# Attention in units of two pairs of heads, with the score matmuls of a pair issued in turn, and the third block's combinations held behind the first expert unit

## The chip, the core and the metric

The kernel runs on one NeuronCore of a Trainium2 chip. Its engines work from queues of their own and wait for one another by semaphores: TensorE (PE, with its weight loads shown as PEld), VectorE (DVE), ScalarE (ACT), GpSimd (POOL), and SyncE (SP), which issues most transfers. The metric is the device time of one execution in microseconds (us).

## What is computed

Three layers follow one another, all in fp32: attention over a band, a gated feed-forward layer, and eight experts of which every token takes a weighted sum.

```python
scores = q @ k.T / sqrt(64) - slope[head] * dist        # 2 batches, 8 heads, 768 tokens
scores = where(is_global | is_local, scores, -1e9)      # the first 8 keys, and the 96 up to the token
a = exp(scores - scores.max(-1)); a = a / (a.sum(-1) + 1e-9)
x = (a @ v)                                             # to 1536 tokens x 512
h = x @ w_in; x = (h * sigmoid(h)) @ w_out              # 512 -> 2048 -> 512
P = exp(x @ w_gate - max); 8 rounds of P /= rows, P /= columns, P *= N / E
for e in range(8): out += P[:, e:e+1] * (maximum(x @ w1[e], 0) @ w2[e])   # 512 -> 1024 -> 512
```

## The kernel before

**Precision.** A product of two fp32 matrices is made of three matmuls of a one-pass format (fp32r): each operand is split into a high part and the rest, and high x high, high x low and low x high are added (`three`, L241 to L243; L280; L407; L442). The high part is made by ScalarE, the rest by VectorE or GpSimd.

**Stages.** The 1536 tokens are three blocks of 512 for the second and third layers, and twelve blocks of 128 queries (k = 0 to 11) for attention. `banded` runs attention for k = 0 and 1 alone, then weaves the rest into the feed-forward layer: k = 2, 3 and then 4 to 7 while the first 512 tokens go through w_in (h, L241) and w_out (y, L280), and k = 8 to 11 while the second 512 do. In the first block VectorE also turns the two weight matrices from 64-bit numbers to fp32 (`narrow`, L203 to L209: 16 pieces of eight operations). `finish` runs the third 512 tokens, and then `layer2` runs the experts.

**An attention unit.** `attention` runs through units; unit (k, j) has the heads 2c + j of all four pairs c, that is one half of every pair. Of a pair the first head's 64 features lie on partitions 0 to 63, the second's on 64 to 127, so all of a unit's score matmuls (`att_scores`, L747) read the same 64 partitions. Two pairs share one PSUM bank of tag "a", of which there are three while attention is woven in; scores, transposes of q and k (L715), of the probabilities (`att_flip`, L785) and the product with v (`att_out`, L804) take turns in them. For blocks 8 to 11 the scores are three fp32r matmuls (kT qT, kTl qT, kT qTl), for the others one fp32 matmul, which the profile shows as two instructions. Then, for each head, VectorE adds the bias and takes the extreme (L756), ScalarE takes the exponential (L760), VectorE makes the reciprocal of the sum (L765, L766), GpSimd multiplies (L768). The flips of a unit come two units later, `att_out` when both units of its block are flipped.

**The experts.** A unit u of `layer2` is one half of an expert's hidden features for one of the three blocks of tokens. Its first matrix is applied by seven products of halves instead of eight (`h_product`, L407), for which the tokens' features are combined beforehand: `x_combine` subtracts quarter tiles (L336) and splits seven of them (L340 on ScalarE, L341 on VectorE), for the first two blocks during the feed-forward layer, and for the third from `rest`, a generator that `window` draws on from unit 1 on. The third block's combinations are needed by unit 2. Within a unit VectorE adds the products' banks (L489, L493, L429) and makes the low parts of what is split (`h_split`, L422); the banks are free for later products when it has read them.

**Order.** The kernel's text gives each instruction a place; a scheduler then sets each engine's order from it by its own estimates, and an instruction that it thinks ready early may stand ahead of its place in the text. Each engine runs its list strictly in order. `tc.issue_after(ins)` holds what is issued in its block behind `ins` on the engine of `ins`, and adds no semaphore.

Of the kernel before, what the change touches and what calls it, by code (L numbers as in the profile page):

```python
# [8 lines left out]
F32 = mybir.dt.float32  # L9
# [11 lines left out]
P = 128  # L21
# [23 lines left out]
def f32(ap):  # L45
    return ap.bitcast(F32)


class Kernel:
# [368 lines left out]
    def h_split(self, src):  # L418

        hi, lo = self.h_room()  # L420
        self.nc.scalar.activation(hi, src, AF.Relu)  # L421
        self.nc.vector.scalar_tensor_tensor(lo, src, 0.0, f32(hi), op0=ALU.max, op1=ALU.subtract)  # L422
        return tuple(x.rearrange("p (f t) -> p f t", f=2) for x in (hi, lo))
# [305 lines left out]
    def att_scores(self, k, j):  # L729
# [5 lines left out]
        jj = slice(j * self.D, (j + 1) * self.D)  # L735
        a["s", j] = s = pool.tile([P, 4, W], F32, tag="s", name=f"s_{k}_{j}", bufs=LAG + 1)
        st = pool.tile([P, 3, 4], F32, tag="st", name=f"st_{k}_{j}", bufs=LAG + 2)
        cols = []
        for c in range(self.NPAIR):
            th = self.tab[2 * c + j]  # L740
            if c % 2 == 0:
                bank = self.aps(f"s_{k}_{j}_{c}")
                for x in (c, c + 1):
                    dst = bank[:, x % 2 * W:x % 2 * W + n]
                    ops = ((0, 0), (0, 1), (1, 0))[:3 if len(qT) > 1 else 1]
                    for i, (y, z) in enumerate(ops):
                        nc.tensor.matmul(  # L747
                            dst, qT[y][jj, x * P:(x + 1) * P], kT[z][jj, x, W - n:],
                            start=i == 0, stop=i == len(ops) - 1,
                        )  # L750
            ps = bank[:, c % 2 * W:c % 2 * W + n]
            tt = th[:, :W] if n == W else th[:, W:]
            sx = s[:, c, W - n:]
            cols.append(sx)

            nc.vector.tensor_tensor_reduce(  # L756
                out=sx, in0=ps, in1=tt, scale=1.0, scalar=BIGMIN, op0=ALU.add, op1=ALU.min,
                accum_out=st[:, 0, c:c + 1],
            )
            nc.scalar.activation(  # L760
                sx, sx, AF.Exp, bias=st[:, 0, c:c + 1], scale=-1.0, accum_out=st[:, 1, c:c + 1]
            )
            if c % 2 == 1:
                two = slice(c - 1, c + 1)
# [423 lines left out]
```

## Time and profile before

| | us |
|---|---|
| median of 3 runs (lowest, highest) | 1426.16 (1425.91, 1428.12) |
| the profiled execution, its own time | 1426.18 |
| its span, first to last instruction | 1424.4 |
| PE busy in the span | 1395.1 (98%) |
| VectorE, ScalarE, GpSimd busy | 731.1, 489.9, 550.9 |

PE is the busiest engine in the mean, but the stages differ: the first 160 us hold attention, the narrowing of the weights and the first block's feed-forward layer, and there VectorE is busy nearly throughout; from then on PE is. The chain that ended last is PE work for 89% of the span. An idle stretch of PE, or work taken from it, is read from the stage in which it lies. The granted clock of PE has two levels here, 2.4 GHz (PEclk 1.0) and 1.2 GHz (0.5).

### The profile page before, as it was taken

How to read it: one execution, taken by the hardware profiler on the slowest of the kernel's cores; microseconds unless marked ns; L12 is line 12 of the kernel's file. 1: busy time of each engine (PE TensorE's matmuls, PEld its weight loads, DVE VectorE, ACT ScalarE, POOL GpSimd, SP SyncE). 2: the span in 40 equal slices, each digit the busy share in tenths (PEclk: the TensorE clock that was granted, in tenths of full speed). 3: DMA queues.
4: the chain of work that ended last, by engine and by line, in shares of the span. 5: the costliest groups of instructions: out<-in, count | busy, mean ns of one | idle time of the engine just before them, and what ended most of it. 6: DMA issues, size and time to landing. Idle time of an engine off the chain costs nothing.

```text
span 1424.4 us, 21277 instructions
## 1 busy us (share of the span) xinstructions
PE 1395.1 (98%) x8552; PEld 1218.0 (86%) x8552; DVE 731.1 (51%) x1298; ACT 489.9 (34%) x949; POOL 550.9 (39%) x489
## 2 busy tenths in 40 slices
PE   8998999999998999999999999999999999999998
PEld 6776677778888998999899989998998899899987
DVE  7899545456235457444444444444444444444443
ACT  6665545555453332222232222222222222222220
POOL 5677756444472424324143331424324142432210
PEclk8999999999999999999999999999999999999999
DMA  9686442212230001010111201011010101101001
GB/s 261 178 249 185 148 119 88 75 61 89 89 110 10 31 30 45 30 45 30 30 30 30 60 16 45 30 30 45 21 55 16 45 31 31 46 30 30 1 31 62
DMA packets 75293, 92.19 MB, mean 65 GB/s; under 512 B 30640, under 2 KB 49072, under 8 KB 75184
## 3 DMA queue, kind: packets, MB, share of 16 engines
q1 hardware_dynamic: 72880, 82.34, 19.3%
q10 hardware_dynamic: 2304, 8.39, 1.5%
q8 instruction: 69, 1.13, 0.3%
q14 instruction: 40, 0.33, 0.1%
HBM read 79.19 MB, written 11.53 MB: 64 GB/s over the span
## 4 chain that ended last, share of the span: by engine, by line
PE 89%; DVE 7%; ACT 1%; issue 1%; POOL 1%; DMA 0%; ACTq 0%; DVEq 0%; SPq 0%; POOLq 0%
PE y L442 37%; PE h L407 32%; PE y L280 8%; PE h L241 3%; PE h L242 3%; PE h L243 3%; PE a_s L747 2%; DVE wf L205 1%; DVE wf L207 1%; PE a_o L804 1%; PE a_f L785 1%; DVE wf L203 1%; DVE wf L209 1%; PE lg L555 0%; DVE st L765 0%
## 5 line engine op out<-in xcount | busy, mean ns | idle before, releaser
L442 PE MATMUL y<-wx1h,room_hh 128*128 128x512 f32 x464 | 181.0, 390 | 0.0
L442 PE MATMUL y<-wx1l,room_hh 128*128 128x512 f32 x464 | 180.9, 390 | 0.0
L442 PE MATMUL y<-wx1h,room_hl 128*128 128x512 f32 x464 | 180.5, 389 | 0.0
L407 PE MATMUL h<-xc,wx0h 128*128 128x256 f32 x1024 | 176.7, 277 | 0.0
L460 DVE SCALAR_TENSOR_TENSOR x<-y,gate,x 128x512 f32<-128x512 f32 x168 | 117.4, 751 | 99.7 <-PE y L442 99.7
L362 POOL TENSOR_TENSOR wx1l<-wf,wx1h 128x512 fp32r<-128x512 f32 x64 | 83.1, 1298 | 208.7 <-ACT wx1h L361 208.6
L407 PEld LDWEIGHTS h<-xc,wx0h 128*128 128x128 f32 x1024 | 154.6, 188 | 0.0
L362 POOL TENSOR_TENSOR wc0l<-wf,wc0h 128x512 fp32r<-128x512 f32 x16 | 21.1, 1320 | 332.8 <-ACT wc0h L361 332.8
L407 PE MATMUL h<-xc,wx0l 128*128 128x256 f32 x512 | 141.8, 277 | 0.0
L421 ACT ACTIVATE room_hh<-tabs 128x512 fp32r<-128x512 f32 x87 | 54.9, 631 | 229.1 <-DVE tabs L429 207.4
L429 DVE TENSOR_TENSOR tabs<-tabs,h 128x512 f32<-128x512 f32 x144 | 94.9, 685 | 37.1 <-PE h L407 35.3
L493 DVE TENSOR_TENSOR tabs<-tabs,h 128x512 f32<-128x512 f32 x48 | 33.0, 687 | 149.0 <-PE h L407 148.8
L442 PE MATMUL y<-wx1h,room_g 128*128 128x512 f32 x304 | 106.0, 389 | 0.0
L442 PEld LDWEIGHTS y<-wx1h,room_hl 128*128 128x128 f32 x464 | 87.1, 188 | 18.3
L442 PEld LDWEIGHTS y<-wx1h,room_hh 128*128 128x128 f32 x464 | 87.1, 188 | 17.3
L442 PEld LDWEIGHTS y<-wx1l,room_hh 128*128 128x128 f32 x464 | 87.1, 188 | 16.9
L407 PEld LDWEIGHTS h<-xc,wx0l 128*128 128x128 f32 x512 | 96.1, 188 | 0.0
L422 DVE SCALAR_TENSOR_TENSOR room_hl<-tabs,room_hh 128x512 fp32r<-128x512 f32 x87 | 69.9, 805 | 42.3 <-ACT room_hh L421 40.5
L225 POOL TENSOR_TENSOR w1l<-wf,w1h 128x512 fp32r<-128x512 f32 x48 | 66.5, 1386 | 50.7 <-ACT w1h L224 41.4
L225 POOL TENSOR_TENSOR w0l<-wf,w0h 128x512 fp32r<-128x512 f32 x48 | 66.7, 1391 | 43.6 <-ACT w0h L224 41.7
L280 PE MATMUL y<-hh,w1h 128*128 128x512 f32 (+1 forms) x208 | 83.0, 399 | 0.0
L280 PE MATMUL y<-hh,w1l 128*128 128x512 f32 (+1 forms) x208 | 78.6, 378 | 0.0
(239 smaller groups left out, 3419.5 us busy)
## 6 DMA issues: line engine op xcount, KB each, us to landing
wf<-in_moe_w_dram SPq DMA_DIRECT2D x64, 512.0 KB, 3.6
wf<-w SPq DMA_DIRECT2D x32, 512.0 KB, 3.2
ra<-in_moe_w_in_dram SPq DMA_DIRECT2D x16, 512.0 KB, 5.7
rb<-in_moe_w_out_dram SPq DMA_DIRECT2D x16, 512.0 KB, 5.0
w<-wf ACTq DMA_DIRECT2D x16, 512.0 KB, 3.7
vw<-in_v_dram SPq DMA_DIRECT2D x8, 448.0 KB, 4.6
qr<-in_q_dram SPq DMA_DIRECT2D x12, 256.0 KB, 5.5
kr<-in_k_dram SPq DMA_DIRECT2D x12, 256.0 KB, 6.1
```

The lines of the kernel that those rows point to most:

```text
L225: nc.gpsimd.tensor_tensor(lo, src, f32(hi), op=ALU.subtract)
L241: nc.tensor.matmul(ps, ah, bh, start=i == 0, stop=False)
L242: nc.tensor.matmul(ps, ah, bl, start=False, stop=False)
L243: nc.tensor.matmul(ps, al, bh, start=False, stop=i == last)
L280: nc.tensor.matmul(self.y[i][:, cols], a, b, start=begin and j == 0, stop=f == self.NF1 - 1 and j == 2, skip_group_check=True,)
L362: self.nc.gpsimd.tensor_tensor(dst[1], src, f32(dst[0]), op=ALU.subtract)
L407: nc.tensor.matmul(ps[:, f * HB:(f + 1) * HB], a[:, k, fs], b[:, k, :], start=first and n == 0, stop=n == 11, skip_group_check=True,)
L421: self.nc.scalar.activation(hi, src, AF.Relu)
L422: self.nc.vector.scalar_tensor_tensor(lo, src, 0.0, f32(hi), op0=ALU.max, op1=ALU.subtract)
L429: self.nc.vector.tensor_tensor(c, a, b, op=op)
L442: nc.tensor.matmul(self.y[i], a, b, start=k == 0 and j == 0, stop=k == 3 and j == 2, skip_group_check=True)
L460: nc.vector.scalar_tensor_tensor(acc, self.y[i], self.gate[:, t, e:e + 1], acc, op0=ALU.mult, op1=ALU.add)
```

## The change

**Attention's units.** Unit (k, m) now has both heads of the pairs 2m and 2m + 1, where it had one head of all four. Its two heads of a pair write to two banks, one for each half j of the partitions, and the score matmuls go by pair, then by product, then by half: neighbours in PE's order read partitions 0 to 63 and 64 to 127 in turn. All twelve (or four) matmuls of a unit are issued before the first reduction, where six (or two) were; both banks are taken at once. The flips and `att_out` follow the new numbering; the order of `att_out`'s matmuls stays.

**The third block's combinations.** `h_split` keeps its last VectorE instruction as `self.mark`; `rest` takes it when it is first drawn on (in unit 1, so it is the last L422 of unit 0) and issues each step of `x_combine` behind it.

```diff
@@ -419,7 +419,7 @@
 
         hi, lo = self.h_room()
         self.nc.scalar.activation(hi, src, AF.Relu)
-        self.nc.vector.scalar_tensor_tensor(lo, src, 0.0, f32(hi), op0=ALU.max, op1=ALU.subtract)
+        self.mark = self.nc.vector.scalar_tensor_tensor(lo, src, 0.0, f32(hi), op0=ALU.max, op1=ALU.subtract)
         return tuple(x.rearrange("p (f t) -> p f t", f=2) for x in (hi, lo))
 
     def h_sum(self, a, b, op):
@@ -726,62 +726,59 @@
                 nc.vector.scalar_tensor_tensor(dst[1], ps, sc, f32(dst[0]), op0=ALU.mult, op1=ALU.subtract)
             yield
 
-    def att_scores(self, k, j):
+    def att_scores(self, k, m):
+
 
         nc, pool = self.nc, self.ap
         a = self.att[k]
         qT, kT = a["qT"], a["kT"]
         n = W if k % self.QT else P
-        jj = slice(j * self.D, (j + 1) * self.D)
-        a["s", j] = s = pool.tile([P, 4, W], F32, tag="s", name=f"s_{k}_{j}", bufs=LAG + 1)
-        st = pool.tile([P, 3, 4], F32, tag="st", name=f"st_{k}_{j}", bufs=LAG + 2)
-        cols = []
-        for c in range(self.NPAIR):
-            th = self.tab[2 * c + j]
-            if c % 2 == 0:
-                bank = self.aps(f"s_{k}_{j}_{c}")
-                for x in (c, c + 1):
-                    dst = bank[:, x % 2 * W:x % 2 * W + n]
-                    ops = ((0, 0), (0, 1), (1, 0))[:3 if len(qT) > 1 else 1]
-                    for i, (y, z) in enumerate(ops):
-                        nc.tensor.matmul(
-                            dst, qT[y][jj, x * P:(x + 1) * P], kT[z][jj, x, W - n:],
-                            start=i == 0, stop=i == len(ops) - 1,
-                        )
-            ps = bank[:, c % 2 * W:c % 2 * W + n]
-            tt = th[:, :W] if n == W else th[:, W:]
-            sx = s[:, c, W - n:]
-            cols.append(sx)
-
-            nc.vector.tensor_tensor_reduce(
-                out=sx, in0=ps, in1=tt, scale=1.0, scalar=BIGMIN, op0=ALU.add, op1=ALU.min,
-                accum_out=st[:, 0, c:c + 1],
-            )
-            nc.scalar.activation(
-                sx, sx, AF.Exp, bias=st[:, 0, c:c + 1], scale=-1.0, accum_out=st[:, 1, c:c + 1]
-            )
-            if c % 2 == 1:
-                two = slice(c - 1, c + 1)
-                nc.vector.tensor_scalar(st[:, 2, two], st[:, 1, two], EPS, None, op0=ALU.add)
-                nc.vector.reciprocal(st[:, 2, two], st[:, 2, two])
-                for y in (c - 1, c):
-                    nc.gpsimd.tensor_scalar(
-                        cols[y], cols[y], st[:, 2, y:y + 1], 1.0, op0=ALU.mult, op1=ALU.mult
+        a["s", m] = s = pool.tile([P, 4, W], F32, tag="s", name=f"s_{k}_{m}", bufs=LAG + 1)
+        st = pool.tile([P, 3, 4], F32, tag="st", name=f"st_{k}_{m}", bufs=LAG + 2)
+        banks = [self.aps(f"s_{k}_{m}_{j}") for j in range(2)]
+        dst = [bank[:, x * W:x * W + n] for x in range(2) for bank in banks]
+        ops = ((0, 0), (0, 1), (1, 0))[:3 if len(qT) > 1 else 1]
+        for x in range(2):
+            c = 2 * m + x
+            for i, (y, z) in enumerate(ops):
+                for j in range(2):
+                    jj = slice(j * self.D, (j + 1) * self.D)
+                    nc.tensor.matmul(
+                        dst[2 * x + j], qT[y][jj, c * P:(c + 1) * P], kT[z][jj, c, W - n:],
+                        start=i == 0, stop=i == len(ops) - 1,
                     )
-                yield
-
-    def att_flip(self, k, j):
+        for x in range(2):
+            for h in (2 * x, 2 * x + 1):
+                th = self.tab[4 * m + h]
+                sx = s[:, h, W - n:]
+
+                nc.vector.tensor_tensor_reduce(
+                    out=sx, in0=dst[h], in1=th[:, :W] if n == W else th[:, W:], scale=1.0, scalar=BIGMIN,
+                    op0=ALU.add, op1=ALU.min, accum_out=st[:, 0, h:h + 1],
+                )
+                nc.scalar.activation(
+                    sx, sx, AF.Exp, bias=st[:, 0, h:h + 1], scale=-1.0, accum_out=st[:, 1, h:h + 1]
+                )
+            two = slice(2 * x, 2 * x + 2)
+            nc.vector.tensor_scalar(st[:, 2, two], st[:, 1, two], EPS, None, op0=ALU.add)
+            nc.vector.reciprocal(st[:, 2, two], st[:, 2, two])
+            for h in (2 * x, 2 * x + 1):
+                sx = s[:, h, W - n:]
+                nc.gpsimd.tensor_scalar(sx, sx, st[:, 2, h:h + 1], 1.0, op0=ALU.mult, op1=ALU.mult)
+            yield
+
+    def att_flip(self, k, m):
 
-        s, blocks = a["s", j], self.blocks(k)
-        at = a["at", j] = pool.tile([P, 8 * P], F32, tag="at", name=f"at_{k}_{j}", bufs=2)
+        s, blocks = a["s", m], self.blocks(k)
+        at = a["at", m] = pool.tile([P, 8 * P], F32, tag="at", name=f"at_{k}_{m}", bufs=2)
...
-                c, o = blocks[n]
-                keys = s[:, c, P:] if o is None else s[:, c, o::2]
+                h, o = blocks[n]
+                keys = s[:, h, P:] if o is None else s[:, h, o::2]
...
@@ -792,19 +789,24 @@
     def blocks(self, k):
 
 
-        return [(c, o) for c in range(self.NPAIR) for o in ((0, 1) if k % self.QT else (None,))]
+        return [(h, o) for h in range(4) for o in ((0, 1) if k % self.QT else (None,))]
 
     def att_out(self, k):
 
         nc = self.nc
         a = self.att.pop(k)
         ps = self.aps(f"o_{k}")
-        for n, (c, o) in enumerate(self.blocks(k)):
-            for j in range(2):
-                nc.tensor.matmul(
-                    ps[j * self.D:(j + 1) * self.D, c * P:(c + 1) * P], a["vw"][:, 2 * c + j, o or 0, :],
-                    a["at", j][:, n * P:(n + 1) * P], start=n == 0, stop=o != 0, skip_group_check=True,
-                )
+        blocks = self.blocks(k)
+        keys = len(blocks) // 4
+        for c in range(self.NPAIR):
+            for o in range(keys):
+                for j in range(2):
+                    n = (c % 2 * 2 + j) * keys + o
+                    nc.tensor.matmul(
+                        ps[j * self.D:(j + 1) * self.D, c * P:(c + 1) * P], a["vw"][:, 2 * c + j, o, :],
+                        a["at", c // 2][:, n * P:(n + 1) * P], start=c + o == 0, stop=o == keys - 1,
+                        skip_group_check=True,
+                    )
         tok = k * P
         xh, xl = (x[:, :, tok % TB:tok % TB + P] for x in self.x1[tok // TB])
         ps = ps.rearrange("p (x c) -> p x c", c=P)
@@ -826,7 +828,7 @@
         if tb not in self.x1:
             self.x1[tb] = self.new_x(f"x1_{tb}")
         ks = range(*SEGS[sg])
-        units = [(k, j) for k in ks for j in range(2)]
+        units = [(k, m) for k in ks for m in range(2)]
         if "qT" not in self.att[ks[0]]:
             yield from self.turn(ks[0])
         none = iter(())
@@ -994,7 +996,13 @@
 
     def rest(self):
         self.gap(self.gp, PAD_R)
-        yield from self.x_combine(self.NB - 1)
+        mark = self.mark.ins
+        combine = self.x_combine(self.NB - 1)
+        more = True
+        while more:
+            with self.tc.issue_after(mark):
+                more = next(combine, self) is not self
+            yield
         yield
         yield from self.gate_logits(self.NB - 1)
         yield from self.gate_parts()
```

PE at the first score unit of block 8, before (names: a_s_8_0_0 is block 8, unit 0, and the bank's first pair; kT, kTl, qT, qTl are the high and low parts of keys and queries; y is the feed-forward layer's second product):

```order
L747 MATMUL a_s_8_0_0_2299<-kT_8_2191,qT_8_2190 128x256
L747 MATMUL a_s_8_0_0_2299<-kTl_8_2193,qT_8_2190 128x256
L747 MATMUL a_s_8_0_0_2299<-kT_8_2191,qTl_8_2192 128x256
L747 MATMUL a_s_8_0_0_2299<-kT_8_2191,qT_8_2190 128x256
L747 MATMUL a_s_8_0_0_2299<-kTl_8_2193,qT_8_2190 128x256
L747 MATMUL a_s_8_0_0_2299<-kT_8_2191,qTl_8_2192 128x256
L280 MATMUL y_0_1_686<-hh_19_2142,w1h_15_2083 128x512
L280 MATMUL y_0_1_686<-hl_19_2143,w1h_15_2083 128x512
L280 MATMUL y_0_1_686<-hh_19_2142,w1l_15_2084 128x512
```

and now (the last number of a_s_8_0_0 and a_s_8_0_1 is the half j):

```order
L746 MATMUL a_s_8_0_0_2299<-kT_8_2191,qT_8_2190 128x256
L746 MATMUL a_s_8_0_1_2300<-kT_8_2191,qT_8_2190 128x256
L746 MATMUL a_s_8_0_0_2299<-kTl_8_2193,qT_8_2190 128x256
L746 MATMUL a_s_8_0_1_2300<-kTl_8_2193,qT_8_2190 128x256
L746 MATMUL a_s_8_0_0_2299<-kT_8_2191,qTl_8_2192 128x256
L746 MATMUL a_s_8_0_1_2300<-kT_8_2191,qTl_8_2192 128x256
L746 MATMUL a_s_8_0_0_2299<-kT_8_2191,qT_8_2190 128x256
L746 MATMUL a_s_8_0_1_2300<-kT_8_2191,qT_8_2190 128x256
L746 MATMUL a_s_8_0_0_2299<-kTl_8_2193,qT_8_2190 128x256
L746 MATMUL a_s_8_0_1_2300<-kTl_8_2193,qT_8_2190 128x256
L746 MATMUL a_s_8_0_0_2299<-kT_8_2191,qTl_8_2192 128x256
L746 MATMUL a_s_8_0_1_2300<-kT_8_2191,qTl_8_2192 128x256
```

The same 96 matmuls of blocks 8 to 11 stand in 8 groups of twelve where they stood in 16 groups of six, and each is followed by one of the other half. Over all blocks the scores stand in 25 groups on PE, where they stood in 45.

VectorE from the end of the feed-forward layer's third block on, before (x_2 is the third block's features, kT_142, qr_89 and kr_91 are the rooms of the combinations, xc the split ones; tabs are the rooms of the experts' sums, h_0_5 is unit 0's second bank):

```order
L293 TENSOR_SCALAR x_2_4219<-y_3_3558 128x512
L336 TENSOR_TENSOR qr_89<-x_2_4219,kT_142 128x512
L336 TENSOR_TENSOR kr_91<-x_2_4219 128x512
L336 TENSOR_TENSOR kT_142<-qr_89,x_2_4219 128x512
L341 TENSOR_TENSOR xc_0xh<-x_2_4219,xc_0xh 128x512
L489 TENSOR_TENSOR tabs<-tabs,h_0_5_4296 128x512
L341 TENSOR_TENSOR xc_0xh<-qr_89,xc_0xh 128x512
L341 TENSOR_TENSOR xc_0xl<-kT_142,xc_0xl 128x512 x2
L341 TENSOR_TENSOR xc_1xh<-kr_91,xc_1xh 128x512
L341 TENSOR_TENSOR xc_1xh<-x_2_4219,xc_1xh 128x512
L341 TENSOR_TENSOR xc_1xl<-x_2_4219,xc_1xl 128x512
L493 TENSOR_TENSOR tabs<-tabs,h_0_5_4296 128x512
```

and now:

```order
L293 TENSOR_SCALAR x_2_4219<-y_3_3558 128x512
L489 TENSOR_TENSOR tabs<-tabs,h_0_5_4296 128x512
L493 TENSOR_TENSOR tabs<-tabs,h_0_5_4296 128x512
L429 TENSOR_TENSOR tabs<-tabs,h_0_4_4310 128x512
L429 TENSOR_TENSOR tabs<-tabs,h_0_3_4323 128x512
L422 SCALAR_TENSOR_TENSOR room_g_4247<-h_0_0_4282,room_g_4246 128x512
L422 SCALAR_TENSOR_TENSOR room_hl_4244<-tabs,room_hh_4241 128x512
L422 SCALAR_TENSOR_TENSOR room_hl_4245<-tabs,room_hh_4242 128x512
L429 TENSOR_TENSOR tabs<-tabs,h_0_4_4310 128x512
L422 SCALAR_TENSOR_TENSOR rooml<-tabs,roomh 128x512
L336 TENSOR_TENSOR kT_142<-x_2_4219 128x512
L489 TENSOR_TENSOR tabs<-tabs,h_1_5_4404 128x512
```

Four combinations (L336) and a low part (L341) stood ahead of the first read of unit 0's second bank (L489), and six low parts between that and the second read (L493). Now the nine sums and low parts of unit 0 come first, and the combinations are spread among those of unit 1. In the first block's stretch VectorE's list keeps its narrowing operations; ahead of the fifteenth gating operation (L261) it has two more reductions (L756, now L755) than before.

## Rows read from the trace of the kernel before

**Rows 1.** The page: shares of the span in the chain that ended last.

```profile
PE 89%; DVE 7%; ACT 1%; issue 1%; POOL 1%; DMA 0%; ACTq 0%; DVEq 0%; SPq 0%; POOLq 0%
```

**Rows 2.** Stretches: length; busy of PE, PEld, DVE, ACT, POOL; PEclk; DMA.

```profile
34.80:159.30 124.50, 110.85 (x652) 86.68 (x652) 115.59 (x254) 77.14 (x194) 88.64 (x90) 0.95 0.65 199
159.30:312.00 152.70, 152.68 (x859) 121.21 (x860) 70.88 (x184) 81.70 (x184) 83.17 (x95) 1.00 0.31 93
...
431.60:435.60 4.00, 0.16 (x2) 0.00 (x0) 3.96 (x5) 0.60 (x1) 3.84 (x3) 1.00 0.00 0
435.60:439.10 3.50, 3.49 (x16) 3.49 (x17) 3.07 (x5) 1.23 (x2) 0.48 (x1) 0.51 0.00 0
```

**Rows 3.** Timeline of PE at a score group (start, us, instruction).

```profile
264.78 0.39 PE L280 MATMUL y<-hl,w1h 128*128 128x512 f32 x1
265.01 0.40 PE L280 MATMUL y<-hh,w1l 128*128 128x512 f32 x1
265.34 0.38 PE L747 MATMUL a_s<-kT,qT 64*128 64x256 f32 x1
265.56 0.28 PE L747 MATMUL a_s<-kTl,qT 64*128 64x256 f32 x1
...
266.04 0.27 PE L747 MATMUL a_s<-kT,qTl 64*128 64x256 f32 x1
266.24 0.50 PE L280 MATMUL y<-hh,w1h 128*128 128x512 f32 x1
266.57 0.39 PE L280 MATMUL y<-hl,w1h 128*128 128x512 f32 x1
```

**Rows 4.** One of three products of the scores in blocks 8 to 11, by form.

```profile
L747 PE MATMUL a_s<-kTl,qT 64*128 64x256 f32 x32 | 8.9, 277 | 0.0
```

**Rows 5.** Timeline of PE, block 0's scores: where units meet, and within one.

```profile
9.94 0.60 PE L747 MATMUL a_s<-kT,qT 64*128 64x128 f32 x6
...
10.60 0.49 PE L747 MATMUL a_s<-kT,qT 64*128 64x128 f32 x3
```

**Rows 6.** Timeline of PE's weight loads where those units meet.

```profile
10.04 0.30 PEld L747 LDWEIGHTS a_s<-kT,qT 64*128 64x128 f32 x4
```

**Rows 7.** Timeline of PE at the last group of fp32 scores.

```profile
165.05 0.39 PE L280 MATMUL y<-hh,w1l 128*128 128x512 f32 x1
165.37 1.13 PE L747 MATMUL a_s<-kT,qT 64*128 64x256 f32 x4
...
166.76 0.40 PE L280 MATMUL y<-hl,w1h 128*128 128x512 f32 x1
```

**Rows 8.** Timeline of PE: the last wait for VectorE in the first block.

```profile
159.32 0.50 PE L241 MATMUL h<-x_0xh,w0h 128*128 128x512 f32 x1 [1.04 <-DVE g L261]
```

**Rows 9.** VectorE's waits in the first 160 us: total, times, longest.

```profile
DVE s L756 <- PE a_s L747: 2.7, 6, 1.2
DVE st L765 <- ACT s L760: 2.4, 3, 0.8
```

**Rows 10.** VectorE's reductions in the first 160 us (busy, mean ns).

```profile
L756 DVE CUSTOM_DVE_ANT_0 s<-a_s,tabs 128x256 f32<-128x256 f32 (+1 forms) x60 | 21.0, 379 | 2.8 <-PE a_s L747 2.7
```

**Rows 11.** Timeline of PE at the start of the experts.

```profile
435.61 0.80 PE L407 MATMUL h<-xc,wc1h 128*128 128x256 f32 x2 [3.85 <-DVE tabs L493]
...
439.14 0.40 PE L407 MATMUL h<-xc,wc0h 128*128 128x256 f32 x2
...
440.55 0.28 PE L407 MATMUL h<-xc,wc1h 128*128 128x256 f32 x1
```

**Rows 12.** Timeline of VectorE there.

```profile
424.21 1.49 DVE L336 TENSOR_TENSOR qr<-x,kT 128x512 f32<-128x512 f32 x1
...
427.44 0.68 DVE L489 TENSOR_TENSOR tabs<-tabs,h 128x512 f32<-128x512 f32 x1
...
434.88 0.68 DVE L493 TENSOR_TENSOR tabs<-tabs,h 128x512 f32<-128x512 f32 x1
435.59 1.28 DVE L429 TENSOR_TENSOR tabs<-tabs,h 128x512 f32<-128x512 f32 x2
```

More of the change, by code (lines that the diff above doesn't have):

```diff
@@ L775, in att_flip @@
+    def att_flip(self, k, m):
         nc, pool = self.nc, self.ap
         a = self.att[k]
-        s, blocks = a["s", j], self.blocks(k)
-        at = a["at", j] = pool.tile([P, 8 * P], F32, tag="at", name=f"at_{k}_{j}", bufs=2)
+        s, blocks = a["s", m], self.blocks(k)
+        at = a["at", m] = pool.tile([P, 8 * P], F32, tag="at", name=f"at_{k}_{m}", bufs=2)
         for lo in range(0, len(blocks), 4):
             hi = min(lo + 4, len(blocks))
-            ps = self.aps(f"f_{k}_{j}_{lo}")
+            ps = self.aps(f"f_{k}_{m}_{lo}")
```

## The prediction

> **What bounds the kernel now.** I read the page first: the chain that ended last is PE for 89% of the span [rows 1], so time is won where PE has less to do or stops waiting, but only in stretches where PE is the engine that is late. The table of stretches sorts that [rows 2]. From 34.8 to 159.3 us VectorE is busy for 115.6 of 124.5 us and PE for 110.9: here VectorE, with the narrowing of the weights and the softmax, sets the pace, and less PE work only lets PE wait longer. From 159.3 to 312 PE is busy for 152.68 of 152.70 us: whatever leaves its list there comes off the end. At 431.6 PE stands still for 4 us while VectorE is busy throughout, and for 3.5 us after that its granted clock is 0.51. The timelines then give the price of each piece.
>
> **Scores of blocks 8 to 11.** They lie in the stretch where PE never waits. One group [rows 3]: the matmuls of y follow at 0.23 us, so without the scores the next would have started at 265.24; the second behind the group starts at 266.57, as if the first had come at 266.34. The group costs 1.10 us. Its scores follow at 0.12 us ((266.04 - 265.56) / 4), so six are 0.72, and 0.38 goes into the change to 64 rows and back. Three products of 32 matmuls [rows 4] are 96, 16 groups of six: 17.6 us. The changed list has 8 groups of twelve, neighbours on different halves of the partitions. If two neighbours run side by side, a group is 0.38 + 6 x 0.12 = 1.10 and all are 8.8: 8.8 us saved. If they run in turn, it is 0.38 + 12 x 0.12 = 1.82, 14.6 in all: 3.0 saved, for the changes of rows alone.
>
> The trace of before shows which of the two. In block 0 a unit on one half is followed directly by one on the other. Three instructions inside a unit take 0.49 us, which with 0.28 for the last one's length [rows 4] is a step of 0.105; six where the units meet take 0.60, three steps and not five [rows 5]. So two pairs ran side by side. Four weight loads there fit into 0.30 us [rows 6], less than three steps before the last one would begin. I take side by side, 8.8.
>
> The Trainium skill (TensorE: Matmul & The Clock Gate, LDWEIGHTS) gives a load as its columns divided by 1.2 GHz, however few the rows, which for 128 columns is an estimate of 0.107 us. If the loads of two halves took turns, a group of twelve would be 0.38 + 12 x 0.107 = 1.66 and the saving 4.3 instead of 8.8. The four loads in 0.30 us speak against the turns. The same page (Packing small matmuls, measured speedup) has 3.07 for four row tiles; half of that for two, an estimate of 1.53, would make the saving 7.0. No group of split scores in this trace has two halves, so neither is ruled out for them.
>
> A unit now holds two of the three banks until four reductions are done, 4 x 0.38 = 1.5 us [rows 10] with small operations between. The next group stands at least 15 matmuls of 0.23, 3.5 us, behind. Only at the second unit of block 8, where the first block's combinations (0.68 each) are queued among the reductions ahead of a gating operation that PE awaits, is the cover about as long as the work. PE now waits for nothing there; the bounds are 0 and a full drain at each of 8 units, 12 us. I take 0.5, near the row that shows no wait.
>
> **Fp32 scores behind the last wait.** PE's last wait for VectorE in the first block ends at 159.32 [rows 8]; two groups of four instructions follow it, and in the new list one of eight. Counted as above, the group takes from 165.05 + 0.23 = 165.28 to 166.76 - 0.23 = 166.53, 1.25 us, of which 0.87 are its four [rows 7]. Side by side the one group costs 1.25 as well: 1.25 saved; in turn 0.4.
>
> **The first 160 us.** The scores of blocks 0 to 7 become shorter on PE, but VectorE's list is the bound and holds the same operations. What can shrink is its idle time: 2.7 us waiting for scores and 2.4 us for exponentials [rows 9]. Half of the first goes with half of PE's time; of the second perhaps 0.5, since more reductions stand between. Against it, two more reductions of 0.38 stand ahead of the fifteenth gating operation: 0.8 later. That is -1.0. The bounds are -5 (all that idle time gone) and +4: an operation of 512 columns takes 0.68 us alone and 1.49 where it meets another engine's [rows 12], and five more such meetings cost 4 us. I take -1.0.
>
> **The start of the experts.** PE stops at 431.6 and resumes at 435.61, its wait put down to L493 [rows 2, 11], which VectorE begins at 434.88, behind the low parts of the third block [rows 12]. That is 4.0 us. The 16 instructions of the next 3.5 us run at half the clock; at full clock twelve take 440.55 - 439.14, 0.118 each, so 16 would take 1.9, and 1.6 more is lost. Both go, 5.6 us, if nothing else is late. With the new order L493 can start when the fifth of six products is done. The sixth takes 12 x 0.118 = 1.4 us and ends at 431.6, so the fifth ends at 430.2; L493 ends at 431.0, the first L429 (0.64) at 431.7, and PE's product that waits for it stands two instructions, 0.24, behind 431.6. At most 0.2 us of waiting stays: 5.4 saved. If each of the two operations takes 1.49 instead, PE waits until 433.2, 1.4 us are lost and 4.2 stay saved. What is late next are the combinations: eleven operations of 0.68 us, 7.5, up to 16 with meetings, spread through unit 1, whose list still has 48 matmuls of 0.23 (11 us) and seven products (10 us) before unit 2 needs them. That hides them. The new hold delays ScalarE's copies that wait for combinations, and behind these the highs of unit 1; those are needed by the second matrix of unit 1, after unit 2's products. GpSimd's combinations of the next weights reuse the rooms and start later, and are first needed in unit 3.
>
> **The sum.** -8.8 + 0.5 - 1.25 - 1.0 - 5.4 = -15.95 us on the profiled execution's 1426.18, which agrees with the median 1426.16: **1410.2 us**.
>
> **Rivals.**
> - The split scores run in turn, because their loads of 128 columns do. For it: the pairs seen were fp32, and every split score of 256 columns brings a load of its own in 0.12 us. Against it: the pairs and their loads [rows 5, 6]. Time: -3.0 + 0.5 - 0.4 - 1.0 - 5.4 = -9.3, 1416.9.
> - The first block gets longer by its bound, +4 instead of -1.0: four reductions in a row delay the narrowing or the gating operations and meet GpSimd more often. For it: VectorE has 93% of that stretch. Against it: the list is the same in kind and number. 1415.2.
> - The stall at the experts comes back in unit 1. There four combinations and two low parts now stand between and ahead of the reads of unit 1's banks (L489, L493); at 0.8 us more each they are 4.8 late, and with the clock the 5.4 are gone: 1415.6. For it: the 1.49 us. Against it: the GpSimd work that they met, busy 3.84 of 4 us in the gap [rows 2], needs their rooms and now comes behind them.
> - Slower: both score banks are held through the reductions, and the third is taken by a transpose, so that PE waits at each unit of blocks 8 to 11. It turns the sign from 2.0 us a unit (15.95 / 8). With a full drain, the gating operation (0.7) and the small ones between, 2.4 us, it is 19: 1429.3. For it: PE's list is in order, and there are three banks; against it: 3.5 us of matmuls lie between, and PE has no wait there now.
>
> **How the numbers follow.** Chances: the forecast 0.71 (its own range 1406.5 to 1414), loads in turn 0.10, the first block longer 0.10, the stall back 0.06, slower 0.03. The range 1404.5 to 1418 takes in the first three rivals and, below, VectorE's idle time gone. Within 0.2% of before, about 2.9 us, cannot be told from no change; it needs two rivals at once, 0.03; slower 0.03; faster 0.94.
>
> **What would show it.** Score starts of blocks 8 to 11 in pairs some ns apart, a group of twelve near 1.1 us from y to y; no PE idle between 159 and 312; no wait on L493 at 431 and no half clock after it; VectorE's first 160 us within a few us of now. Wrong would be: groups of 1.8 us; PE waits on L755 or L261 in the second block; a wait of some us in unit 1.

## The result, and the profile after

The changed kernel takes 1407.04 us (median of 4 runs, 1404.97 to 1407.46) against 1426.04 for the kernel before (4 runs, 1424.93 to 1428.12). The ratio is 0.986, its 95% interval 0.9845 to 0.9876. The forecast was 1410.2. The profiled execution takes 1407.18 us with a span of 1405.3.

The chain that ended last is PE for as much of the span as before [rows 1]:

```profile
PE 89%; DVE 9%; issue 1%; ACT 1%; DMA 0%; POOL 0%; ACTq 0%; DVEq 0%; SPq 0%
```

Four stretches tell where the time went; they begin at the first product behind the first block's last gating operation (L241), at the product behind the last fp32 block's `att_out` (L804, now L805), at the first product of the experts (L407) and at the first of their second matrices (L442). Columns as in [rows 2]. Before:

```profile
159.32:169.03 9.71, 9.71 (x52) 6.85 (x52) 4.80 (x19) 7.05 (x19) 7.83 (x10) 1.00 0.45 147
169.03:423.12 254.09, 253.09 (x1306) 202.80 (x1305) 114.37 (x228) 125.84 (x254) 135.68 (x130) 1.00 0.30 92
423.12:447.14 24.02, 20.18 (x157) 19.97 (x156) 18.54 (x24) 7.87 (x15) 7.79 (x5) 0.93 0.07 23
447.14:1424.39 977.25, 971.90 (x6222) 879.93 (x6220) 450.68 (x682) 250.23 (x412) 291.10 (x222) 1.00 0.11 34
```

and after:

```profile
155.79:164.10 8.31, 8.31 (x53) 6.17 (x51) 2.83 (x13) 5.54 (x14) 6.47 (x9) 1.00 0.53 193
164.10:409.66 245.56, 244.52 (x1307) 197.25 (x1306) 113.47 (x227) 124.81 (x254) 135.73 (x130) 1.00 0.31 95
409.66:427.85 18.19, 18.19 (x158) 18.14 (x156) 11.01 (x18) 7.96 (x15) 1.47 (x2) 1.00 0.10 30
427.85:1405.30 977.45, 972.10 (x6222) 880.04 (x6220) 458.13 (x688) 249.99 (x412) 297.31 (x226) 1.00 0.11 34
```

| stretch | before, after (us) | measured | forecast |
|---|---|---|---|
| up to the product behind the last gating operation | 159.32, 155.79 | -3.5 | -1.0 |
| the fp32 groups behind it | 9.71, 8.31 | -1.4 | -1.25 |
| up to the experts (blocks 8 to 11) | 254.09, 245.56 | -8.5 | -8.8 + 0.5 |
| start of the experts | 24.02, 18.19 | -5.8 | -5.4 |
| the rest | 977.25, 977.45 | +0.2 | 0 |

The rows differ by 19.1 us, the profiled executions by 19.0. The first stretch is the one that moved otherwise than forecast.

A group of twelve scores on PE after, where [rows 3] has one of six:

```profile
249.78 0.40 PE L243 MATMUL h<-x_1xh,w0l 128*128 128x512 f32 x1
250.11 0.39 PE L746 MATMUL a_s<-kT,qT 64*128 64x256 f32 x2
250.33 0.28 PE L746 MATMUL a_s<-kTl,qT 64*128 64x256 f32 x2
250.45 0.28 PE L746 MATMUL a_s<-kT,qTl 64*128 64x256 f32 x2
...
250.80 0.28 PE L746 MATMUL a_s<-kT,qTl 64*128 64x256 f32 x2
...
251.35 0.39 PE L242 MATMUL h<-x_1xl,w0h 128*128 128x512 f32 x1
```

Each row is now two matmuls, with one step of 0.12 us to the next row. From 249.78 + 0.23 to 251.35 - 0.23 the group takes 1.11 us, as long as one of six did. The last fp32 group [rows 7] is one of eight instructions in the time of four:

```profile
156.26 0.39 PE L243 MATMUL h<-x_0xh,w0l 128*128 128x512 f32 x1
156.58 1.13 PE L746 MATMUL a_s<-kT,qT 64*128 64x256 f32 x8
157.64 0.50 PE L241 MATMUL h<-x_0xh,w0h 128*128 128x512 f32 x1
```

VectorE at the start of the experts, where [rows 12] had combinations and low parts ahead of L493:

```profile
412.75 0.69 DVE L489 TENSOR_TENSOR tabs<-tabs,h 128x512 f32<-128x512 f32 x1 [2.21 <-PE h L407]
416.92 0.69 DVE L493 TENSOR_TENSOR tabs<-tabs,h 128x512 f32<-128x512 f32 x1 [3.48 <-PE h L407]
```

and PE there [rows 11]:

```profile
418.13 0.40 PE L407 MATMUL h<-xc,wc1h 128*128 128x256 f32 x2
418.38 0.51 PE L407 MATMUL h<-xc,wc2h 128*128 128x256 f32 x2
```

VectorE now waits for PE, L493 follows the fifth product at once, and PE goes from one product to the next without a gap; PEclk of the whole stretch is 1.00.

VectorE's waits in the first 156 us, for [rows 9] (total, times, longest):

```profile
DVE st L763 <- ACT s L759: 1.2, 3, 0.6
```

No wait for scores is left (2.7 before), and that for exponentials is halved.

At the end of that stretch another engine is late now. VectorE's last gating operation, before and then after:

```profile
158.58 0.69 DVE L261 SCALAR_TENSOR_TENSOR g<-g,h 128x512 f32<-128x512 f32 x1 [0.45 <-ACT g L260]
```

```profile
153.44 0.69 DVE L261 SCALAR_TENSOR_TENSOR g<-g,h 128x512 f32<-128x512 f32 x1 [0.60 <-ACT g L260]
```

VectorE is there 5.1 us earlier. Before, PE's product begins 0.05 us behind that operation, at 159.32 [rows 8]; after, it begins 1.66 us behind it, at 155.79, and PE has not waited for it: its last wait in the block is one of 2.45 us that ends at 150.23, and from there it works without a gap, at a PEclk of 0.69:

```profile
150.23 0.66 PE L782 MATMUL a_f<-ident,s 128*128 128x128 f32 x4 [2.45 <-DVE x_1xl L814]
```

```profile
150.23:155.79 5.56, 5.56 (x20) 4.45 (x20) 3.28 (x14) 4.22 (x13) 3.44 (x7) 0.69 0.00 0
```

From 151.20 to 154.61 us the granted clock is 0.50. By estimate, full clock in these 3.41 us would save half of them, 1.7 us, which is what PE is late.

### The profile page after: what moved, and what is told of

Read it like the earlier page. It is cut to its first block, busy times and chain, and to the rows that moved or that the text cites. A ratio compares the mean times of both kernels' runs of the same rounds, so it can differ in the third digit from the quotient of the medians.

```text
span 1405.3 us, 21277 instructions
## 1 busy us (share of the span) xinstructions
PE 1375.1 (98%) x8552; PEld 1205.5 (86%) x8552; DVE 728.6 (52%) x1298; ACT 487.8 (35%) x949; POOL 555.0 (39%) x489
## 3 DMA queue, kind: packets, MB, share of 16 engines
q8 instruction: 69, 1.13, 0.3%
## 4 chain that ended last, share of the span: by engine, by line
PE 89%; DVE 9%; issue 1%; ACT 1%; DMA 0%; POOL 0%; ACTq 0%; DVEq 0%; SPq 0%
PE y L442 37%; PE h L407 33%; PE y L280 7%; PE h L241 3%; PE h L242 2%; PE h L243 2%; DVE wf L205 2%; PE a_o L805 1%; DVE wf L203 1%; DVE wf L207 1%; DVE wf L209 1%; DVE s L755 1%; PE a_f L782 1%; DVE st L763 1%; DVE g L261 0%
## 5 line engine op out<-in xcount | busy, mean ns | idle before, releaser
L442 PE MATMUL y<-wx1h,room_hh 128*128 128x512 f32 x464 | 181.0, 390 | 0.0
L442 PE MATMUL y<-wx1l,room_hh 128*128 128x512 f32 x464 | 180.8, 390 | 0.0
L442 PE MATMUL y<-wx1h,room_hl 128*128 128x512 f32 x464 | 180.5, 389 | 0.0
L407 PE MATMUL h<-xc,wx0h 128*128 128x256 f32 x1024 | 176.5, 277 | 0.0
L407 PEld LDWEIGHTS h<-xc,wx0h 128*128 128x128 f32 x1024 | 154.5, 188 | 0.1
L407 PE MATMUL h<-xc,wx0l 128*128 128x256 f32 x512 | 141.6, 277 | 0.0
L493 DVE TENSOR_TENSOR tabs<-tabs,h 128x512 f32<-128x512 f32 x48 | 33.0, 688 | 150.3 <-PE h L407 150.3
L442 PE MATMUL y<-wx1h,room_g 128*128 128x512 f32 x304 | 106.0, 389 | 0.0
L442 PEld LDWEIGHTS y<-wx1h,room_hl 128*128 128x128 f32 x464 | 87.1, 188 | 18.4
L442 PEld LDWEIGHTS y<-wx1h,room_hh 128*128 128x128 f32 x464 | 87.1, 188 | 17.3
L442 PEld LDWEIGHTS y<-wx1l,room_hh 128*128 128x128 f32 x464 | 87.1, 188 | 16.9
L407 PEld LDWEIGHTS h<-xc,wx0l 128*128 128x128 f32 x512 | 96.1, 188 | 0.0
L422 DVE SCALAR_TENSOR_TENSOR room_hl<-tabs,room_hh 128x512 fp32r<-128x512 f32 x87 | 70.5, 811 | 41.5 <-ACT room_hh L421 40.0
L767 POOL TENSOR_SCALAR s<-s,st 128x256 f32<-128x256 f32 (+1 forms) x96 | 67.1, 711 | 36.0 <-DVE st L764 12.1
```

What stands on the lines that cost most here:

```text
L407: nc.tensor.matmul(ps[:, f * HB:(f + 1) * HB], a[:, k, fs], b[:, k, :], start=first and n == 0, stop=n == 11, skip_group_check=True,)
L422: self.mark = self.nc.vector.scalar_tensor_tensor(lo, src, 0.0, f32(hi), op0=ALU.max, op1=ALU.subtract)
L442: nc.tensor.matmul(self.y[i], a, b, start=k == 0 and j == 0, stop=k == 3 and j == 2, skip_group_check=True)
L493: nc.vector.tensor_tensor(u3, s1, b2, op=ALU.add)
L767: nc.gpsimd.tensor_scalar(sx, sx, st[:, 2, h:h + 1], 1.0, op0=ALU.mult, op1=ALU.mult)
```

## The experiments

The theory at this point: two matmuls on different halves run side by side; a change to 64 rows and back costs 0.38 us a group; the hold takes the stall at the experts away by itself; and the first block gains where VectorE no longer waits. The end of the first block is told, in the expectations too, by the product behind its last gating operation; that is called a last wait there, but in the changed kernel PE doesn't wait at it. The rivals: fewer groups explain the gain without any pairs; and the first block's gain is chance or belongs to the order of the lists. Each kernel was timed in five rounds beside the kernel before, whose medians were 1425.9 to 1427.1 us.

**The attention part alone.** The edit puts `yield from self.x_combine(self.NB - 1)` back into `rest`.

> The attention part alone; the third block's combinations stand where they stood before. Theory (the parts are independent): only the stretch at the start of the experts changes against the changed kernel. PE waits there again for L493 some 4 us and then works about 3.5 us at half clock, so the time is 1407.0 + 5.8 = 1412.8, and the span up to the first h2 of the experts stays as in the changed kernel (409.7 us or a few us more). Rival (part of the gain at the experts comes from the attention part, because VectorE arrives there earlier in relation to PE): less than 3 us of it comes back, below 1410.

Measured: 1413.66 us, ratio 0.9913 (0.9898 to 0.9928). The wait of PE returns, and with it the half clock:

```profile
PE h L407 <- DVE tabs L493: 3.8, 1, 3.8
```

Its stretches up to the experts and at their start:

```profile
164.67:410.23 245.56, 244.52 (x1307) 197.24 (x1306) 114.50 (x228) 124.81 (x254) 135.72 (x130) 1.00 0.30 95
410.23:435.10 24.87, 21.02 (x158) 20.82 (x156) 18.54 (x24) 7.87 (x15) 7.81 (x5) 0.86 0.08 22
```

The second block takes the changed kernel's 245.56 to the hundredth; the experts' start, at a PEclk of 0.86, is 6.7 us longer than its 18.19, and 0.85 longer than before. So 6.6 us come back, where 5.8 were expected.

**The hold alone.**

```diff
-        yield from self.x_combine(self.NB - 1)
+        mark = self.mark.ins
+        combine = self.x_combine(self.NB - 1)
+        more = True
+        while more:
+            with self.tc.issue_after(mark):
+                more = next(combine, self) is not self
+            yield
...
```

`h_split` keeps its mark as in the change.

> The kernel before with the hold of the third block's combinations alone. Theory: the 4 us of waiting and the 1.6 us at half clock go, and a wait of at most some tenths takes their place: 1426.0 - 5.4 to 5.8 = 1420.4. Rival (the stall comes back in unit 1, or the rest of the layer gives it back): 1423 or more. The first 420 us should be as in the kernel before, within the variation of its first block.

Measured: 1420.01 us, ratio 0.9959 (0.9945 to 0.9973), 5.9 less than before.

```profile
168.31:422.40 254.09, 253.11 (x1307) 202.80 (x1305) 114.23 (x227) 125.82 (x254) 135.71 (x130) 1.00 0.30 92
422.40:440.59 18.19, 18.19 (x157) 18.13 (x156) 11.00 (x18) 7.96 (x15) 1.47 (x2) 1.00 0.09 31
```

The two parts are independent: but for the 0.85 us more at the start of the experts without the hold, each stretch has the length of the kernel whose part it carries, the first block within 0.7 us. The stall does not come back in unit 1.

**The changed kernel again.**

> The changed kernel once more, for the variation of the first block from run to run. Three profiles of kernels with the pairs have the last wait of the first block end at 155.8, 156.4 and 156.4 us of the span, two without at 159.3 and 158.6. Theory (the gain of the first block is real, 2.7 us): again 155.5 to 156.8, and 1407.0 in all. Rival (the 155.8 was a lucky run): 158 or more.

Measured: 1407.09 us, ratio 0.9868 (0.9853 to 0.9883); the product behind the first block's last gating operation begins at 156.2, and the second block takes 245.55. So a stretch bound by PE repeats within some hundredths, the first block within some tenths.

**Split scores by half, in sixes.** In `att_scores` the twelve are sorted by half:

```diff
+        turns = [(x, i, j) for x in range(2) for i in range(len(ops)) for j in range(2)]
+        if len(ops) > 1:
+            turns.sort(key=lambda e: e[2])
+        for x, i, j in turns:
...
```

> The changed kernel, with the split scores of blocks 8 to 11 ordered by half: six matmuls of the first half of the partitions, then six of the second; groups, banks and everything behind them stay. Theory (neighbours on different halves run side by side): only one neighbouring pair is left in a group, which takes 0.38 + 11 x 0.12 = 1.70 us instead of 1.10, so 8 groups cost 4.8 us more: 1411.8. Rival (the gain in blocks 8 to 11 comes from fewer groups and the new places, and the order of the halves is no matter): 1407, no change.

Measured: 1409.67 us, ratio 0.9883 (0.9868 to 0.9899). Neither theory had that: the second block takes 248.07, 2.5 more than after, where 4.8 or 0 were expected. The group shows why:

```profile
251.80 0.40 PE L243 MATMUL h<-x_1xh,w0l 128*128 128x512 f32 x1
252.12 0.38 PE L747 MATMUL a_s<-kT,qT 64*128 64x256 f32 x1
252.35 0.27 PE L747 MATMUL a_s<-kTl,qT 64*128 64x256 f32 x1
252.46 0.28 PE L747 MATMUL a_s<-kT,qTl 64*128 64x256 f32 x1
252.47 0.39 PE L747 MATMUL a_s<-kT,qT 64*128 64x256 f32 x2
...
253.17 0.27 PE L747 MATMUL a_s<-kT,qTl 64*128 64x256 f32 x1
...
253.70 0.39 PE L242 MATMUL h<-x_1xl,w0h 128*128 128x512 f32 x1
```

The row of 252.47 holds two products kT qT. One half's next matmul follows at 0.12 us; what begins there 0.01 us behind the third matmul is the second half's first, seventh in the list, ahead of three that stand before it. Three of each half then run side by side, nine steps are left of twelve, and the group takes 253.47 - 252.03 = 1.44. All eight groups of this run have these nine steps.

**In threes.** Within each pair, three products of the first half and then three of the second:

```diff
+            turns = [(i, j) for i in range(len(ops)) for j in range(2)]
+            if len(ops) > 1:
+                turns.sort(key=lambda e: e[1])
+            for i, j in turns:
...
```

> The changed kernel, with the split scores of blocks 8 to 11 in threes: three matmuls of the first half, three of the second, three of the first, three of the second. The run in sixes took 1.44 us a group, since the first matmul of the second half began beside the third of the first half, ahead of three that stand before it. Theory (PE begins a matmul of the other half while up to three of the first half are still to begin): in threes the other half is always near enough, a group takes 1.10 to 1.2 us, and the time is 1407.0 to 1408. Rival (the overlap in sixes belongs to the end of a half's list only, so that between threes about two of three steps are lost): a group near 1.44 again, 1409.7; a second rival (only direct neighbours run side by side, three places in a group of twelve): 9 of 12 steps, 1.46, the same 1409.7.

Measured: 1407.72 us, ratio 0.9874 (0.9859 to 0.989). All six steps are pairs again, and the second block takes 245.93:

```profile
250.16 0.40 PE L243 MATMUL h<-x_1xh,w0l 128*128 128x512 f32 x1
250.48 0.39 PE L748 MATMUL a_s<-kT,qT 64*128 64x256 f32 x2
...
251.18 0.28 PE L748 MATMUL a_s<-kT,qTl 64*128 64x256 f32 x2
...
251.73 0.39 PE L242 MATMUL h<-x_1xl,w0h 128*128 128x512 f32 x1
```

The fourth of the list starts with the first. So the halves need not alternate one by one.

**Groups of twelve without pairs.** Units of one half as before, with the hold, all twelve issued at once into two banks:

```diff
-            if c % 2 == 0:
-                bank = self.aps(f"s_{k}_{j}_{c}")
-                for x in (c, c + 1):
-                    dst = bank[:, x % 2 * W:x % 2 * W + n]
+            if c == 0:
+                banks = [self.aps(f"s_{k}_{j}_{x}") for x in (0, 2)]
+                for x in range(self.NPAIR):
+                    dst = banks[x // 2][:, x % 2 * W:x % 2 * W + n]
...
```

> The kernel before with the hold of the third block's combinations, and with all twelve (or four) score matmuls of a unit issued at once into two banks, but the units still of one half: groups as in the changed kernel, no neighbour on another half. Theory (0.38 us per group, the rest by the pairs): a group is 0.38 + 12 x 0.12 = 1.82, so against the kernel with the hold alone the second block saves 8 x 0.38 = 3.0 and the fp32 group behind the last wait 0.4; the first 155 us stay near that kernel's 158.6, since PE's score time stays: 1416.6. Rival (the first block's gain of 2.7 comes from four reductions standing together and fewer groups, not from PE's shorter scores): the first block ends near 156, 1413.9. A second rival (fewer groups give nothing): 1420.

Measured: 1416.05 us, ratio 0.9928 (0.9913 to 0.9943). A group:

```profile
256.52 0.40 PE L243 MATMUL h<-x_1xh,w0l 128*128 128x512 f32 x1
256.84 0.39 PE L747 MATMUL a_s<-kT,qT 64*128 64x256 f32 x1
...
258.80 0.39 PE L242 MATMUL h<-x_1xl,w0h 128*128 128x512 f32 x1
```

It takes 258.57 - 256.75 = 1.82 us, as worked out, and the second block 250.84, 3.25 less than 254.09 with the hold alone. The last wait of the first block ends at 158.4, near the 158.6 there: grouping alone, with the places that it brings, gives the first block nothing that can be seen.

**Pairs in groups of six.** The first pair's reductions stand between the two pairs' score matmuls: the second `for x in range(2):` of `att_scores` goes, and its body follows the matmuls in the first.

> The changed kernel, with the second pair's score matmuls issued behind the first pair's reductions, so that PE meets the scores of blocks 8 to 11 in 16 groups of six as before, each still with neighbours on different halves. Theory (each group costs 0.38 us for the change to 64 rows and back, and a pair of matmuls 0.12): a group is 0.38 + 3 x 0.12 = 0.74, 16 are 11.8 against 8.8, so +3.0 in the second block, +0.4 for the fp32 groups behind the last wait: 1410.4, if the first 155 us stay. Rival (fewer groups give nothing, since the change of rows is paid per matmul): no change in the second block, 1407. A second rival: the second pair's matmuls wait for the first pair's reductions, which would be seen as waits of PE in blocks 8 to 11 and cost more than 3 us.

Measured: 1420.86 us, ratio 0.9962 (0.9949 to 0.9976), 10 us more than the theory gave. Its part on the second block holds: a group of six in pairs takes

```profile
262.20 0.40 PE L243 MATMUL h<-x_1xh,w0l 128*128 128x512 f32 x1
262.53 0.39 PE L746 MATMUL a_s<-kT,qT 64*128 64x256 f32 x2
...
263.41 0.39 PE L242 MATMUL h<-x_1xl,w0h 128*128 128x512 f32 x1
```

0.75 us, and the second block 249.11, 3.6 more than after (3.0 forecast). But the first block ends at 165.5. A second pair's scores, whose banks the first pair's reductions read, wait there for these, and VectorE then waits for the scores (waits up to 165.5 us, the first row PE's weight loads):

```profile
PEld a_s L746 <- DVE st L754: 3.6, 6, 1.6
DVE s L754 <- PE a_s L746: 11.9, 14, 2.0
```

PE's granted clock up to there is 0.85 of full speed, after 0.89, and this run doesn't tell what each of the two costs. The second rival named the right cause in the wrong block: in blocks 8 to 11 PE waits for reductions once, for 0.2 us.

**Fp32 scores by half.** The sort of the sixes, for blocks 0 to 7 alone (`len(ops) == 1`).

> The changed kernel, with the fp32 scores of blocks 0 to 7 ordered by half (two matmuls, four instructions, of the first half, then as many of the second), the split ones in turn as in the changed kernel. By the overlap seen in sixes, most of a group of eight instructions can still run side by side, so PE's score time grows little, 0.1 to 0.4 us a group. Theory (the first block is bound by VectorE and gains from shorter scores only where VectorE waits for them): the end of the first block moves by at most 1 us, 1407.0 to 1408.2. Rival (PE's score time in the first block sets its length): 12 groups x 0.4 = 4.8 us, 1411.8. VectorE's order in the first block differs in places here, which is a third cause that this run can't exclude.

Measured: 1412.8 us, ratio 0.9906 (0.9892 to 0.9919). The second block is unchanged at 245.55, and the product behind the first block's last gating operation begins at 161.4. PE's scores up to there, in the columns PE, PEld and DVE, are as long as after. After, and then this run:

```profile
10.00:155.80 145.80, 19.69 (x120) 11.94 (x120) 20.47 (x60) 0.89 0.73 222
```

```profile
10.00:161.40 151.40, 19.97 (x116) 12.33 (x112) 21.09 (x60) 0.89 0.71 213
```

19.97 us against 19.69, where the kernel before has 30.8 up to 159.3. So neither the theory (at most 1 us) nor the rival (longer scores) holds: with equal scores the block is 5.6 us longer. What differs is the place of the operations in the lists, VectorE's, ScalarE's and GpSimd's among them, which the scheduler made differently: VectorE begins the last gating operation at 160.18 instead of 153.44, and 2.6 us of waits for scores are back.

**VectorE with less to do.** `nc.vector.tensor_scalar(st[:, 2, two], st[:, 1, two], EPS, ...)` is taken out, and the reciprocal reads `st[:, 1, two]`. The addition of 1e-9 is left out.

> The changed kernel without the addition of 1e-9 to the sum of the exponentials (L763 of the changed kernel; the sum holds exp(0), so in fp32 the addition rounds to nothing); the reciprocal reads the sum directly. It takes 30 operations off VectorE's list before the last wait of the first block, which are busy 10.3 us there (0.34 each), and whose successors often begin 0.08 us behind their start. Theory (VectorE's busy time plus its idle time is the length of the first block, whatever PE does there): the last wait ends 2.4 (30 x 0.08) to 8 us earlier than 156, as long as VectorE's idle stays near 5 us; the middle, 4 us, makes 1403. Rival (the order of the list decides more than its content, as the 161.4 us of the run with the fp32 scores by half suggest): VectorE's idle time grows by what is taken off, 1407 or above. The second block should keep its 245.6 us.

Measured: 1409.65 us, ratio 0.9877 (0.9858 to 0.9896). Stretches of all engines up to the product behind the last gating operation, after and then without the addition (DVE is the third of the busy times):

```profile
10.00:155.80 145.80, 123.89 (x776) 95.78 (x775) 138.29 (x334) 97.28 (x254) 111.46 (x114) 0.89 0.73 222
```

```profile
10.00:158.00 148.00, 121.65 (x775) 94.88 (x773) 134.90 (x303) 95.93 (x250) 109.25 (x109) 0.90 0.70 215
```

and VectorE's longest wait without it:

```profile
DVE s L755 <- PE a_s L746: 7.7, 3, 6.0
```

VectorE does 3.4 us less and stands idle for 13.1 us (148.00 - 134.90) instead of 7.5. One wait for scores is 6.0 us long: PE itself had waited 3.45 us for a part of w_in from GpSimd just before, and then, at half clock, the eight score instructions of the unit took 2.09 us, where eight take 1.13 at full clock.

**One reciprocal for four heads, without the addition.** `nc.vector.reciprocal(st[:, 2, :], st[:, 1, :])` once a unit; the addition is left out here too.

> As the run without the addition, and with one reciprocal for the four heads of a unit where there are two: 45 operations fewer on VectorE before the last wait of the first block than in the changed kernel. Theory (VectorE's list is the length of the first block): 15 more x 0.08 = 1.2 us earlier than in the run without the addition alone, if the exponentials of four heads are done when the reciprocal's turn comes. Rival (VectorE, which works in order, waits at the reciprocal for the last of four exponentials, 16 units x up to 0.8 us): up to 10 us later than that run.

Measured: 1409.67 us, ratio 0.9872 (0.9853 to 0.9892).

```profile
10.00:158.70 148.70, 122.23 (x772) 95.88 (x770) 131.22 (x288) 95.92 (x249) 107.50 (x109) 0.89 0.70 214
```

7.1 us less work than after on VectorE, 10 us more idle time. The theory that its work is the length of the block falls with both runs. The rival's wait for four exponentials isn't seen either, 0.2 us in all; VectorE's longest waits are for ScalarE's high part of x_0 (6.5 us, three times). Neither kernel beats the changed one.

## Why the prediction was right, point by point

The profiled execution came out 3.05 us under the sum, and 2.5 of them lie in the first block, the one term that was badly sized.

**Scores of blocks 8 to 11 (-8.8, waits +0.5): right in mechanism and size.** The four kernels with and without pairs, in groups of six and twelve, give the second block 254.1 (six, apart), 250.8 (twelve, apart), 249.1 (six, pairs) and 245.6 us (twelve, pairs). Dropping eight groups is worth 3.3 to 3.6, the pairs 5.0 to 5.3; the forecast had 3.0 and 5.8. The rival that split scores run in turn would have left a group near 1.82; it is 1.11. The estimate of 1.66 us for a group of twelve is not borne out: two loads and two matmuls share each step of 0.12. It took the length of a load from the Trainium skill (TensorE: Matmul & The Clock Gate, LDWEIGHTS). That loads of two halves take turns was the prediction's own condition, and it is this that fails. The ratio of 3.07 for four row tiles that the Trainium skill gives on that page (Packing small matmuls, Measured speedup), halved as an estimate, was too low for two: six pairs take 0.72 us, as six single matmuls did, a ratio of 2. That the 0.38 us of a group come from the change to 64 rows fits the timeline after, though no run varies the rows: four flips of 128 rows (L782) between two products of w_in take 125.25 - 0.23 - (124.31 + 0.23) = 0.48 us, 0.12 each, which leaves nothing for a change. The wait for two banks, for which 0.5 stood, cannot be seen; what PE waits for there, 1.0 us at L241, is in the kernel before as well.

**Fp32 group (-1.25): right**, 1.4.

**First 160 us (-1.0): the mis-sized term.** In this pair of profiles it is -3.5. With the five kernels that share the changed kernel's lists up to there (155.8, 156.2, 155.8, 156.4, 156.4) against the two that share the list of before (159.3, 158.6), it is -2.8. Two steps were off, in opposite directions. The first is "half of the first goes with half of PE's time": up to the last gating operation VectorE's idle time fell from 148.58 - 137.13 = 11.45 us

```profile
10.00:158.58 148.58, 132.09 (x769) 100.76 (x768) 137.13 (x328) 95.05 (x246) 105.21 (x111) 0.91 0.72 216
```

to 6.17 at equal work:

```profile
10.00:153.44 143.44, 121.53 (x768) 93.92 (x767) 137.27 (x331) 95.25 (x248) 110.10 (x111) 0.90 0.75 225
```

All of the 2.7 us of waiting for scores went, and the run with equal score time but other places has it back. The second is that PE would follow VectorE's list: PE took back 1.6 of the 5.1 us at half clock. All five kernels with these lists have PE 1.5 to 2.6 us behind the last gating operation, the two with the list of before 0.05.

But idle time and work don't add up to a fixed law. The other four of the five do 140.9 to 141.0 us of work up to PE's product and are idle for 4.9 to 5.4, where the changed kernel's profile has 138.3 and 7.5, and they end within 0.6 us of it; the kernel with the hold alone waits 1.0 us for scores where the kernel before waits 2.7, with the same list, and ends 0.7 us earlier; and less work gave more idle time. The block is a loop of four engines, and the place of the operations in their lists can move it by 5.6 us at equal score time. How much of the 2.8 comes from shorter scores and how much from places stays open, since no run shortened the scores and kept the lists.

**Start of the experts (-5.4): right**, 5.8 to 6.7. The 0.2 us of waiting that were kept did not appear, and the clock did not fall; the combinations in unit 1 cost at most some tenths, since the rest of the layer is 0.2 us longer after and 0.4 longer with the hold alone.

**The slower rival**, PE waiting at each unit of blocks 8 to 11 for banks, did not occur: PE is busy for 244.52 of 245.56 us.

## What to carry to other kernels

Price a group of small matmuls from neighbour to neighbour, not from its own rows: here 0.38 us of each group was the change of rows, and the rest halved when the other half of the partitions stood within three places in PE's list. In a stretch where PE never waits such a price came out to tenths; in one where several engines wait for one another, give the scheduler's new order a range of its own (here 155.8 to 165.5 us for much the same work), don't expect work taken off the busiest engine to shorten it, and look at the granted clock at its end before you say which engine sets it. An operation that needs nothing yet, queued ahead of one that frees a bank, cost here its wait of 3.8 us and then 3.4 or 5.3 us of PE's work at half clock, of which half, 1.7 or 2.7 us, is lost by estimate.

## What the runs showed of the hardware that was not expected

- PE began a matmul of the other half while three of the first half that stand before it had not begun (252.47 us in the run in sixes), but not earlier than that, in any of the eight groups. In threes, with two before it, the second half began with the first, 0.01 us later. So on PE a list is not run strictly in order, as was said of every engine ahead of the prediction.
- Two split matmuls of 64 rows on different halves, side by side, cost what one does: 0.12 us a step either way.
- PE waits 3.8 us at the start of the experts both before and in the run of the attention part alone, but the granted clock is half from 435.63 to 439.04 us in the one, from the end of the wait on, and from 421.21 to 428.04 in the other, where the wait ends at 422.71: 3.4 and 5.3 us of work at half clock. The stretch took 24.02 and 24.87 us. What sets the length of the half clock is not shown.
